# Transposing row blocks by DMA instead of on TensorE, in the prologue and in the z stage

## Chip, cores and metric
The kernel runs on one core of a Trainium2 chip. Its time is the device time of one execution in microseconds (us), lower being better. Before the change the median of three executions is 1714.83 us.

## What is computed
One transformer block on x (2048 x 512, float32): layer norm, 32-head attention (16 columns a head) with a residual, then layer norm and a gated MLP whose gate mixes over the sequence. `_A_ref` is the attention, `_B_ref` the MLP:

```python
qkv = transpose((x @ wqkv).reshape(B, S, 3, H, Dh), 2, 0, 3, 1, 4)   # x here is layernorm(x)
p = softmax(einsum("bhqd,bhkd->bhqk", q, k) * Dh ** -0.5, axis=-1)
o = einsum("bhqk,bhkd->bhqd", p, v)          # then @ wo, and h = x + ...
...
z = gelu(einsum("bsd,df->bsf", x, w_in))     # x here is layernorm(h)
z1 = z[..., :Fh]                             # Fh = 688
z2 = layernorm(z[..., Fh:], axis=-1)
g = einsum("ts,bsf->btf", w_sp, z2) + b_sp[None, :, None]
return einsum("bsf,fd->bsd", z1 * g, w_out)  # and h + ... is the result
```

## The kernel before
Products that need more precision than fp16 run as three fp16 matmuls: each operand is split in a high and a low fp16 half, and `mm3` (L106 to L109) multiplies high by high, high by low and low by high. A 128-row block of an operand therefore has to be there transposed and in two halves.

The span has four stages. The **prologue** (0 to about 165 us) loads x in 16 row blocks (`load_x`), takes statistics on DVE (`stats`), works out the scales (`scales`: one 1/sqrt chain for four blocks, ending in `nb`), normalizes on ACT (`normal`, L412), transposes on TensorE (`turn_only`, L424: four 128x128 transposes a block into PSUM) and splits (`put_x`: ACT copies the high half, L433, DVE subtracts the low half, L431). xT holds the halves. `proj_v(sb)` projects one block to v (12 matmuls of 0.216 us, 2.6 us) and `proj_qk(0, g, t)` four blocks to a q or k part; their results are taken by DVE or ACT during the next projection and stored by SyncE (v_scr, k_scr, q_scr, uv_scr). The loop over g = 0, 1, 2 treats blocks 4 to 15 in fours: it projects v of blocks 4g to 4g+3 and readies blocks 4g+4 to 4g+7. `load_q` loads the first q rows for attention (qst, six DMAs); `load_wqk` loads weights (wg).

**Attention** (about 165 to 1294 us) runs 512 units n of scores, exponentials and weighted sums; h for the first rows is made in its last units. **z** (about 1294 to 1452 us) goes over the 16 rows (blocks) in the order `h_rows`; in iteration k TensorE makes h of row k+2 (`make_h`, L747, 12 matmuls), then z of row k (`make_z`, 48 matmuls through `mm3`), with four transposes of LN(h) of row k+1 (`turn`, L1177) among them, which ACT (L98) and DVE (L104) split. `load_o` (L723, L726, L729) loads attention's output o, the softmax's 1/sums rc and the row xr of x; POOL multiplies o by rc (L731), ACT and DVE split it (`split_o`, L737, L740). h lands in xr (L751) and is stored in h_scr (L752). LN(h) is hn: applied by ACT (L1271) with scale and bias from a 1/sqrt chain (`rstd_of` with one column, L114 to L126). LN of z's second half has a chain of its own in `gate_z`, after which ACT applies it (L1214) and ACT, POOL and DVE write the sums and halves that the final stage multiplies (`parts`). The **final stage** (about 1452 to 1712 us) multiplies by w_sp and w_out.

In the prologue, attention and z, `manual_schedule` makes program order the order of each engine's queue. All DMAs that SyncE and ACT issue rotate over eight semaphores, so that a DMA waits, at its issue, for the one eight places earlier. Everything queued behind a waiting instruction on its engine waits with it.

Of the kernel before, what the change touches and what calls it, by code (L numbers as in the profile page):

```python
# [19 lines left out]
P = 128  # L20
S = 2048
# [38 lines left out]
def block_kernel(ctx: ExitStack, tc: tile.TileContext, x, wqkv, wo, w_in, w_sp4, b_sp, w_out, out):  # L60
# [208 lines left out]
    with ExitStack() as pre:  # L269
# [7 lines left out]
        xT = [pc.tile([P, DB, S], F16, name=f"xT{i}") for i in range(2)]  # L277
# [148 lines left out]
        def put_x(sb, *which):  # L426

            c = slice(sb * P, (sb + 1) * P)
            for i in which:
                if i:  # L430
                    nc.vector.tensor_sub(xT[1][:, :, c], tps[sb], xT[0][:, :, c])  # L431
                else:
                    nc.scalar.activation(xT[0][:, :, c], tps[sb], AF.Copy)  # L433

        def turn_x(*blocks):

# [175 lines left out]
        for g in range(3):  # L612
            a, b = 4 * g, 4 * g + 4
            mv = moments(4)
            if g:
                proj(proj_v, a)
                turn_x(a + 2, a + 3)
                if g == 1:
                    load_x(14)
                    load_x(15)  # L620
                stats(mv, b, b + 1)
                proj(proj_v, a + 1)
                stats(mv, b + 2, b + 3)
                proj(proj_v, a + 2)
                normal = scales(mv)
                normal(b, b + 1)
                proj(proj_v, a + 3)
            else:
                proj(proj_v, 2, on_act=True)
                stats(mv, 4, 5, 6)  # L630
                measures.pop(0)()
                stats(mv, 7)
                put_wqk(0)
                proj(proj_v, 3, on_act=True)
            if g == 1:
                load_q(0)
            proj(proj_qk, 0, g, 1)
            if not g:
                normal = scales(mv)
                normal(b, on="dve")  # L640
                normal(b + 1)
            if g == 2:
                load_wqk(1)
            proj(proj_qk, 0, g, 0, then=lambda: turn_x(b, b + 1), at=1 if g else 2)
            if not g:
                load_x(12)
                load_x(13)
            normal(b + 2, b + 3)
        weigh_wqk(1)
        proj(proj_v, 12)  # L650
        turn_x(14, 15)
        load_wqk(2)
        load_wqk(3)
        measures.pop(0)()
# [61 lines left out]
    os_, o2s, xrs, hns, hTs = {}, {}, {}, {}, {}  # L716

    def load_o(sb):

        c = slice(sb * P, (sb + 1) * P)  # L720
        o = e2.tile([P, DB, P], F32, name="o")
        for d in range(DB):
            nc.sync.dma_start(o[:, d, :], o_scr[d, :, :DH, c])  # L723
        rc = e2.tile([P, DB, P], F32, name="rc")
        for d in range(DB):
            nc.sync.dma_start(rc[:, d, :], r_scr[8 * d:8 * d + 8, c].rearrange(  # L726
                "h (o s) -> h o s", o=1).to_broadcast([8, DH, P]))
        xrs[sb] = e2.tile([P, D], F32, name="xr", bufs=3)
        nc.sync.dma_start(xrs[sb], x[c, :])  # L729
        os_[sb] = o  # L730
        return lambda: nc.gpsimd.tensor_mul(o, o, rc)  # L731

# [27 lines left out]

    def new_hn(sb):
        mv, rs = scale_h(sb)
        hns[sb] = e2.tile([P, D], F32, name="hn", bufs=3)
        nc.vector.tensor_scalar(hns[sb], xrs.pop(sb), mv[:, 0:1], rs, op0=ALU.subtract, op1=ALU.mult)

    def minus_mean(pool, mv, rs):
        nb = pool.tile([P, 1], F32, name="nb")
# [20 lines left out]
    with ExitStack() as at:  # L788
# [256 lines left out]
        for n in range(0, len(units), 2):  # L1045
# [85 lines left out]
                invert()  # L1131
            if n in (474, 484, 504, 508):
                asked.append(load_o(h_rows[{474: 0, 484: 1, 504: 2, 508: 3}[n]]))
            if n in (484, 492, 508):
                asked.pop(0)()
            if len(later) == 1 or n in (498, 510):
# [2 lines left out]
                steps_h.append(make_h(h_rows[1], later[0].tile([P, 512], F32, name="h")))  # L1139
            if n == 502:  # L1140
                new_hn(h_rows[0])
        weigh(*prev)
        take(*prev[:2], e2)
        asked.append(load_o(h_rows[4]))
# [21 lines left out]
    with ExitStack() as mid:  # L1166
        m2 = mid.enter_context(tc.tile_pool(name="mid_2", bufs=2))
        zs, zst = {}, {}
        ps = mid.enter_context(tc.tile_pool(name="mid_ps", bufs=5, space=PSUM))
        pt = mid.enter_context(tc.tile_pool(name="mid_pt", bufs=2, space=PSUM))  # L1170

        def turn(sb):

            hn = hns.pop(sb)
            tp = pt.tile([P, DB, P], F32, name="tp")
            for d in range(DB):
                nc.tensor.transpose(tp[:, d, :], hn[:, d * P:(d + 1) * P], ident)  # L1177
            hTs[sb] = [m2.tile([P, DB, P], F16, name=f"hT{i}") for i in range(2)]
            split(hTs[sb][0], hTs[sb][1], tp, "act")

        def new_z(sb):
            zs[sb] = [m2.tile([P, FH], F32, name=f"z{i}", bufs=1 + 3 * i) for i in range(2)]
# [17 lines left out]
            else:  # L1200
                sub(nc.gpsimd if el == "pool" else nc.vector)

        subs, put_off = [], []

        def gate_z(sb, meanwhile):

            z = zs.pop(sb)
            rows = slice(sb * P, (sb + 1) * P)
            nc.scalar.dma_start(z_scr[rows, :], z[0])
            mv = m2.tile([P, 2], F32, name="zmv")  # L1210
            nc.vector.bn_aggr(mv, zst.pop(sb))
            rs = rstd_of(m2, mv[:, 1:2], 1, up=Z2_UP)
            nb = minus_mean(m2, mv, rs)
            nc.scalar.activation(z[1], z[1], AF.Identity, bias=nb, scale=rs)  # L1214
            zs[sb] = z[1]
            meanwhile()
# [12 lines left out]
            t2 = m2.tile([P, FC], F32, name="t2", bufs=1)  # L1229
            e.tensor_sub(t2, b22, t1)  # L1230
            parts("t2", k, t2, eh, el)
            parts("b22", k, b22, "pool" if last else "act", "pool")
            nc.gpsimd.tensor_sub(b12, b22, b12)
            parts("t3", k, b12, "pool", "pool")
            parts("b21", k, b21, "pool" if last else "act", "pool" if last else "later")
            nc.gpsimd.tensor_sub(t2, b21, t2)
            parts("n4", k, t2, "pool", "pool")

        row = dict(enumerate(h_rows))
        with tc.manual_schedule(engines={E.PE, E.Activation, E.DVE, E.Pool, E.SP}):  # L1240
            asked.pop(0)()
            turn(row[0])
            new_hn(row[1])
            for k in range(NB):
                sb, new = row[k], row.get(k + 2)
                if new is not None:
                    for _ in make_h(new, ps.tile([P, 512], F32, name="acc")):
                        pass
                if k + 3 < NB:
                    split_o(row[k + 3])  # L1250
                new_z(sb)
                make_z(sb, 1, 0)
                if k + 1 < NB and k != NB - 2:
                    turn(row[k + 1])
                if new is not None:
                    mv, rs = scale_h(new)
                    nb = minus_mean(e2, mv, rs)
# [11 lines left out]
                if new is not None:  # L1269
                    hns[new] = e2.tile([P, D], F32, name="hn", bufs=3)  # L1270
                    nc.scalar.activation(hns[new], xrs.pop(new), AF.Identity, bias=nb, scale=rs)  # L1271
                if k == 1:
                    invert()
                if k >= NB - 8:
                    ask()

                def meanwhile(k=k):
                    if k + 4 < NB:
                        asked.pop(0)()
                    if k + 5 < NB:  # L1280
                        asked.append(load_o(row[k + 5]))

                if k == NB - 3:
                    put_off.append(lambda sb=sb, then=meanwhile: gate_z(sb, then))
                else:
                    gate_z(sb, meanwhile)
    early.close()
    late.close()

# [314 lines left out]
```

## Time and profile before

| | |
|---|---|
| median of three runs (lowest, highest) | 1714.83 us (1714.73, 1715.37) |
| span of the profiled execution | 1712.3 us |
| its own time | not listed apart from the span; the median lies 2.5 us above the span |
| granted TensorE clock, whole span | 1.000 |
| prologue / attention / z / final stage | about 165 / 1129 / 158 / 260 us |
| busy: PE, DVE, ACT, POOL | 1699.5, 1452.5, 1317.5, 813.6 us |

The profile counts an engine as busy while an instruction of it runs; matmuls overlap, so that of a run of matmuls the distance between starts is the price. A row of the waits says who waited, at which line, for whom, and for how long in total, how many times, and the longest. SPq is SyncE's queue: the time in which it issues a DMA, not the transfer.

### The profile page before, as it was taken

Reading aid. Unit: us, or ns where it says so; the run is one execution under the profiler, and the core shown is the slowest. Engines: PE = TensorE matmul, PEld = TensorE weight load, DVE = VectorE, ACT = ScalarE, POOL = GpSimd, SP = SyncE. Lnnn points to the kernel's source line nnn. Section 1 sums busy time; section 2 is a strip of 40 time slices with the busy share of each in tenths; the row PEclk is TensorE's granted clock in tenths of the full one; section 3 lists DMA queues with packets and bytes.
Section 4 is the critical chain, followed back from the end, with each engine's and each line's share of the span. In section 5 each row is a group of like instructions: output and inputs, shape, how many; then the busy total and the mean of one; then the engine's idle time right before and its main releaser. Section 6 shows DMA issues by size and latency. Waiting matters only on the chain.

```text
span 1712.3 us, 36689 instructions
## 1 busy us (share of the span) xinstructions
PE 1699.5 (99%) x13508; PEld 644.7 (38%) x13508; DVE 1452.5 (85%) x3051; ACT 1317.5 (77%) x2584; POOL 813.6 (48%) x1062
## 2 busy tenths in 40 slices
PE   9999999999999999999999999999999999999999
PEld 4533222222222222222222222222225666656665
DVE  7688999999999999999999999999936787543444
ACT  4334999999999999999999999999995545211111
POOL 1231867776673267687767776400002766300100
PEclk9999999999999999999999999999999999999999
DMA  5534332342221244344434444300114454664551
GB/s 185 167 94 144 103 89 68 101 94 82 81 68 25 56 118 117 104 144 125 130 113 124 132 140 130 80 13 19 37 39 124 140 173 140 233 234 156 198 217 44
DMA packets 189309, 196.03 MB, mean 114 GB/s; under 512 B 67496, under 2 KB 140008, under 8 KB 189128
## 3 DMA queue, kind: packets, MB, share of 16 engines
q1 hardware_dynamic: 186824, 188.04, 36.8%
q10 hardware_dynamic: 2304, 5.64, 0.8%
q8 instruction: 106, 1.74, 0.4%
q14 instruction: 75, 0.61, 0.1%
HBM read 122.10 MB, written 65.93 MB: 110 GB/s over the span
## 4 chain that ended last, share of the span: by engine, by line
PE 78%; DVE 12%; DMA 3%; POOL 2%; ACT 2%; SPq 2%; issue 1%; ACTq 0%; POOLq 0%; DVEq 0%
PE pv L830 26%; PE s L805 17%; PE m L223 9%; DVE mx L228 7%; PE acc L107 4%; PE g L108 4%; PE g L109 4%; PE g L107 4%; PE acc L109 4%; PE acc L108 4%; DMA rc<-r_scr 1%; DVE ab L237 1%; DVE og L840 1%; SPq L723 1%; DVE rs_t L124 1%
## 5 line engine op out<-in xcount | busy, mean ns | idle before, releaser
L814 ACT ACTIVATE pt<-s 128x512 f32<-128x512 f32 x1968 | 1006.2, 637 | 5.5 <-PE m L223 4.3
L228 DVE TENSOR_REDUCE mx<-m 128x1 f32<-128x512 f32 x1510 | 947.5, 682 | 11.7 <-PE m L223 2.9
L805 PE MATMUL s<-qst,kst 50*128 50x512 f16 x2048 | 604.2, 379 | 0.2
L830 PE MATMUL pv<-pt,vst 128*32 128x256 f32 (+1 forms) x6056 | 598.1, 466 | 4.1 <-DVE og L840 1.3
L223 PE MATMUL m<-kst,qst 48*128 48x512 f16 x1510 | 452.4, 381 | 0.0
L805 PEld LDWEIGHTS <-kst 50*128 50x128 f16 x2048 | 132.0, 94 | 352.1 <-issue 323.7
L830 PEld LDWEIGHTS pv<-pt,vst 128*32 128x32 f32 x6056 | 119.5, 108 | 290.7 <-issue 277.3
L223 PEld LDWEIGHTS <-qst 48*128 48x128 f16 x2048 | 159.2, 93 | 173.6 <-issue 124.2
L223 PE MATMUL m<-uvs,qst 48*128 48x512 f16 x504 | 190.5, 380 | 0.6 <-DVE mx L228 0.6
L245 POOL TENSOR_SCALAR nm<-nm 128x16 f32<-128x16 f32 x32 | 6.6, 206 | 358.8 <-DVE nm L242 358.8
L237 DVE CUSTOM_DVE_ANT_0 ab<-m,ab 128x512 f32<-128x512 f32 x252 | 170.5, 677 | 2.7 <-ACT ab L233 2.7
L233 ACT ACTIVATE ab<-m 128x512 f32<-128x512 f32 x252 | 157.3, 624 | 15.5 <-PE m L223 14.8
L1368 ACT ACTIVATE pr<-pr,up 128x304 f32<-128x304 f32 (+1 forms) x32 | 17.0, 574 | 109.2 <-DVE up L1322 109.2
L991 POOL TENSOR_TENSOR op<-raw,op 128x512 f16<-128x512 f32 x80 | 92.9, 1161 | 6.0
L914 POOL TENSOR_TENSOR raw<-raw 128x512 f32<-128x512 f32 (+1 forms) x84 | 83.3, 991 | 6.7
L919 POOL TENSOR_TENSOR acc_sp<-acc_sp,raw 128x512 f32<-128x512 f32 x63 | 80.4, 1277 | 4.5
L109 PE MATMUL acc<-wi,hT 128*128 128x344 f16 x256 | 79.1, 309 | 0.3 <-DVE hT L104 0.3
L107 PE MATMUL acc<-wi,hT 128*128 128x344 f16 x256 | 79.1, 309 | 0.0
L108 PE MATMUL acc<-wi,hT 128*128 128x344 f16 x256 | 79.1, 309 | 0.0
L1510 POOL TENSOR_TENSOR pr<-pr,z 128x344 f32<-128x344 f32 x8 | 7.3, 914 | 145.9 <-DMA whole<-squares 108.3
L911 POOL TENSOR_SCALAR raw<-raw 128x512 f32<-128x512 f32 (+1 forms) x88 | 52.3, 594 | 19.7 <-DMA raw<-in_wqkv 12.4
L1509 DVE TENSOR_TENSOR pr<-g,v 128x344 f32<-128x344 f32 x8 | 4.1, 517 | 66.6 <-PE g L109 63.5
(247 smaller groups left out, 2292.9 us busy)
## 6 DMA issues: line engine op xcount, KB each, us to landing
raw<-in_w_sp SPq DMA_DIRECT2D x128, 256.0 KB
s_scr<-op SPq DMA_DIRECT2D x64, 256.0 KB
op<-s_scr SPq DMA_DIRECT2D x32, 512.0 KB
a_scr<-op SPq DMA_DIRECT2D x48, 256.0 KB
op<-a_scr SPq DMA_DIRECT2D x24, 512.0 KB
o_scr<-og SPq DMA_DIRECT2D x64, 128.0 KB
qst<-q_scr SPq DMA_DIRECT2D x192, 32.0 KB
kst<-k_scr SPq DMA_DIRECT2D x48, 128.0 KB
```

Source lines behind the costliest of these rows:

```text
L107: nc.tensor.matmul(ps, lh, rh, start=first, stop=False, **kw)
L108: nc.tensor.matmul(ps, lh, rl, start=False, stop=False, **kw)
L109: nc.tensor.matmul(ps, ll, rh, start=False, stop=last, **kw)
L223: nc.tensor.matmul(acc, q[r, p, c], keys[r, p], start=True, stop=True)
L228: nc.vector.reduce_max(at(t, e if t else e - 1), acc, axis=AX.X)
L233: nc.scalar.activation(ab[0], acc, AF.Abs)
L237: nc.vector.tensor_tensor_reduce(ab[0], acc, ab[0], 0.5, LOW, ALU.add, ALU.max, at(0, 0))
L805: nc.tensor.matmul(s, kst[hg % 2][r, p, kb * P:(kb + 1) * P], qst[hg * NQ + qb][r, p, :], start=True, stop=True)
L814: nc.scalar.activation(pts[p, kb][:, t, :], s, AF.Exp, scale=scales_[hg // 2])
L830: nc.tensor.matmul(pv[0][32 * j:32 * j + 32, a:b], vst[hg % 2][:, c:c + 32], pts[j % 2, kb][:, j // 2, a:b], start=kb == 0, stop=kb == NB - 1,
L914: pool.tensor_mul(got[0] if n else acc, got[0], got[0])
L991: chores.append((lambda: pool.tensor_sub(t[0][:, 1], of(), t[0][:, 0]), TT))
```

## The change
In the prologue blocks 8 to 15 are no longer transposed on TensorE. ACT copies the normalized block into the first half of an fp16 tile xp, POOL subtracts for the second half, and one transposing DMA, issued by SyncE, writes all eight 128x128 pieces into xT (`split_x`). The statistics come as three blocks and one, and the scales ahead of proj_v(a + 2); `load_wqk(1)` moves to the start of g = 2.

In z the same is done to LN(h): `halve_h` copies (ACT; DVE for the first row), `turn_h` subtracts on DVE and issues the transposing DMA into hT. Row 0's is done at unit n = 504 of attention, row 1's ahead of the loop, row k+1's at the start of iteration k. One chain, `scale_both`, serves z of row k and h of row k+2. The gate of row k−1 comes in iteration k, z's first half is stored right after it is made, xr is loaded by itself, and the z matmuls have seven PSUM buffers instead of five.

```diff
+        def split_x(*blocks):
+            for sb in blocks:
+                xn = xns.pop(sb)
+                xp = p2.tile([P, 2, D], F16, name="xp", bufs=4)
+                nc.scalar.activation(xp[:, 0], xn, AF.Copy)
+                nc.gpsimd.tensor_sub(xp[:, 1], xn, xp[:, 0])
+                nc.sync.dma_start_transpose(
+                    xTs[:, :, :, sb * P:(sb + 1) * P].rearrange("p i d s -> p (i d) s"),
+                    xp.rearrange("p i c -> p (i c)"))
...
             if g:
+                if g == 2:
+                    load_wqk(1)
                 proj(proj_v, a)
-                turn_x(a + 2, a + 3)
                 if g == 1:
+                    turn_x(a + 2, a + 3)
                     load_x(14)
                     load_x(15)
-                stats(mv, b, b + 1)
+                stats(mv, b, b + 1, b + 2)
                 proj(proj_v, a + 1)
-                stats(mv, b + 2, b + 3)
+                stats(mv, b + 3)
+                normal = scales(mv)
+                for sb in (b, b + 1):
+                    normal(sb)
+                    split_x(sb)
                 proj(proj_v, a + 2)
-                normal = scales(mv)
-                normal(b, b + 1)
+                for sb in (b + 2, b + 3):
+                    normal(sb)
+                    split_x(sb)
                 proj(proj_v, a + 3)
...
+    def turn_h(sb):
+        hp = hps.pop(sb)
+        nc.vector.tensor_sub(hp[:, 1], hns.pop(sb), hp[:, 0])
+        t = e2.tile([P, 2 * DB, P], F16, name="hT")
+        nc.sync.dma_start_transpose(t, hp.rearrange("p i c -> p (i c)"))
+        hTs[sb] = [t[:, :DB], t[:, DB:]]
...
             for k in range(NB):
                 sb, new = row[k], row.get(k + 2)
+                if k and k + 1 < NB:
+                    nb, rs = scaled.pop(row[k + 1])
+                    hns[row[k + 1]] = e2.tile([P, D], F32, name="hn")
+                    nc.scalar.activation(hns[row[k + 1]], xrs.pop(row[k + 1]), AF.Identity, bias=nb, scale=rs)
+                    halve_h(row[k + 1])
+                    turn_h(row[k + 1])
...
+                if k:
+                    gate_z(row[k - 1])
                 new_z(sb)
                 make_z(sb, 1, 0)
-                if k + 1 < NB and k != NB - 2:
-                    turn(row[k + 1])
...
                 make_z(sb, 1, 1)
-                if k == NB - 2:
-                    turn(row[k + 1])
-                    put_off.pop()()
                 for c in range(2):
                     nc.vector.bn_stats(zst[sb][:, c, :], zs[sb][1][:, c * FC:(c + 1) * FC])
+                scale_both(new, sb)
                 make_z(sb, 0, 0)
                 make_z(sb, 0, 1)
+                nc.scalar.dma_start(z_scr[sb * P:(sb + 1) * P, :], zs[sb][0])
```

The order on SyncE's queue in the prologue, from the last load of x on; names are destination and source (v_scr, k_scr, q_scr and uv_scr are stores of projections, qst attention's first rows of q, wg weights). Before:

```order
L286 DMA xg<-in_x 128x512 x2
L493 DMA v_scr<-v 128x512 x3
L194 DMA qst<-q_scr 16x2x512 x6
L493 DMA v_scr<-v 128x512
L464 DMA k_scr<-part 128x2x512
L481 DMA uv_scr<-part 64x2x512 x2
L464 DMA q_scr<-part 128x2x512
L493 DMA v_scr<-v 128x512 x4
L345 DMA wg<-in_wqkv 128x4x128 x2
```
The same queue after, from the same place on:

```order
L505 DMA v_scr<-v 128x512
L443 DMA_TRANSPOSE xT<-xp 128x8x128 x2
L505 DMA v_scr<-v 128x512
L443 DMA_TRANSPOSE xT<-xp 128x8x128 x2
L505 DMA v_scr<-v 128x512
L194 DMA qst<-q_scr 16x2x512 x6
L505 DMA v_scr<-v 128x512
L476 DMA k_scr<-part 128x2x512
L346 DMA wg<-in_wqkv 128x4x128 x2
L493 DMA uv_scr<-part 64x2x512 x2
L476 DMA q_scr<-part 128x2x512
L505 DMA v_scr<-v 128x512
```
Four transposing DMAs (blocks 8 to 11) now stand ahead of qst, and those of blocks 12 to 15 follow the last row shown, in two pairs with a v_scr between.

SyncE's queue in one iteration of z, before:

```order
L752 DMA h_scr<-xr 128x512
L723 DMA o<-o_scr 128x1x128 x4
L726 DMA rc<-r_scr 128x1x128 x4
L729 DMA xr<-in_x 128x512
L752 DMA h_scr<-xr 128x512
```
and after:

```order
L799 DMA_TRANSPOSE hT<-hp 128x8x128
L772 DMA h_scr<-xr 128x512
L738 DMA xr<-in_x 128x512
L745 DMA o<-o_scr 128x1x128 x4
L748 DMA rc<-r_scr 128x1x128 x4
L799 DMA_TRANSPOSE hT<-hp 128x8x128
```
The transposing DMA stands first in the iteration, and xr has moved ahead of o and rc.

ACT's queue in one iteration of z (tp is the transposes' PSUM, acc the z matmuls', fig a scale), before:

```order
L737 ACTIVATE o_20883<-o,fig_1844 128x512
L1192 ACTIVATE z_20888<-acc,fig_1841 128x344
L98 ACTIVATE hT_20909<-tp 128x512
L1192 ACTIVATE z_20888<-acc,fig_1841 128x344
L1192 ACTIVATE z_20887<-acc,fig_1841 128x344 x2
L1271 ACTIVATE hn<-xr,nb,rs_u 128x512
L1214 ACTIVATE z_20888<-z_20888,nb,rs_u 128x688
```
and after:

```order
L1296 ACTIVATE hn<-xr,nb_21163,r_21161 128x512
L790 ACTIVATE hp<-hn 128x512
L757 ACTIVATE o_21229<-o,fig_1819 128x512
L1261 ACTIVATE z_21122<-z_21122,nb_21163,r_21161 128x688
L1226 CAST b_0_20646<-z_21122 128x344
L1226 CAST b_0_20644<-z_21122 128x344
L1222 ACTIVATE z_21260<-acc,fig_1816 128x344 x2
L1222 ACTIVATE z_21259<-acc,fig_1816 128x344 x2
L1324 DMA z_scr<-z_21259 128x688
```
hn and its copy now open the iteration, the gate of the row before follows, and the store of z's first half, issued by ACT, closes it.

More of the change, by code (lines that the diff above doesn't have):

```diff
@@ L275, in block_kernel @@
         more[3] = more[4] = lambda: pt.tile([P, 512], F32, name="tp")
-        xT = [pc.tile([P, DB, S], F16, name=f"xT{i}") for i in range(2)]
+        xTs = pc.tile([P, 2, DB, S], F16, name="xT")
+        xT = [xTs[:, i] for i in range(2)]
         wv = [pc.tile([P, DB, D], F16, name=f"wv{i}") for i in range(2)]
@@ L637, in block_kernel @@
             proj(proj_qk, 0, g, 1)
-            if not g:
+            if g:
+                proj(proj_qk, 0, g, 0)
+            else:
                 normal = scales(mv)
@@ L641, in block_kernel @@
                 normal(b + 1)
[L642 to L645, printed above, removed]
+                proj(proj_qk, 0, g, 0, then=lambda: turn_x(b, b + 1), at=2)
                 load_x(12)
                 load_x(13)
-            normal(b + 2, b + 3)
+                normal(b + 2, b + 3)
         weigh_wqk(1)
         proj(proj_v, 12)
-        turn_x(14, 15)
         load_wqk(2)
@@ L715, in block_kernel, with load_row @@
     h_rows = [0, 1, HB, HB + 1] + [sb + HB * i for sb in range(2, HB) for i in range(2)]
-    os_, o2s, xrs, hns, hTs = {}, {}, {}, {}, {}
+    os_, o2s, xrs, hns, hps, hTs = {}, {}, {}, {}, {}, {}
+    def load_row(sb):
+        xrs[sb] = e2.tile([P, D], F32, name="xr", bufs=3)
+        nc.sync.dma_start(xrs[sb], x[sb * P:(sb + 1) * P, :])
     def load_o(sb):
@@ L762, in new_hn, with halve_h @@
         mv, rs = scale_h(sb)
-        hns[sb] = e2.tile([P, D], F32, name="hn", bufs=3)
+        hns[sb] = e2.tile([P, D], F32, name="hn")
         nc.vector.tensor_scalar(hns[sb], xrs.pop(sb), mv[:, 0:1], rs, op0=ALU.subtract, op1=ALU.mult)
+    def halve_h(sb, on_act=True):
+        hps[sb] = e2.tile([P, 2, D], F16, name="hp")
+        if on_act:
+            nc.scalar.activation(hps[sb][:, 0], hns[sb], AF.Copy)
+        else:
+            nc.vector.tensor_copy(hps[sb][:, 0], hns[sb])
+    def turn_h(sb):
[4 more added lines that the diff above has]
+        hTs[sb] = [t[:, :DB], t[:, DB:]]
     def minus_mean(pool, mv, rs):
@@ L1168, in block_kernel @@
         zs, zst = {}, {}
[L1169 to L1179, printed above, removed]
+        ps = mid.enter_context(tc.tile_pool(name="mid_ps", bufs=7, space=PSUM))
         def new_z(sb):
@@ L1201, in parts, with scale_both, gate_z @@
                 sub(nc.gpsimd if el == "pool" else nc.vector)
[L1203 to L1213, printed above, removed]
+        subs = []
+        def scale_both(new, sb):
+            n = 1 if new is None else 2
+            mv = m2.tile([P, 2, 2], F32, name="mv2")
+            hv = m2.tile([P, 2], F32, name="hv2")
+            for i, (row, stats, up) in enumerate(((sb, zst, Z2_UP), (new, hst, HN_UP))[:n]):
+                nc.vector.bn_aggr(mv[:, i, :], stats.pop(row))
+                nc.vector.tensor_scalar(hv[:, i:i + 1], mv[:, i, 1:2], EPS, 0.5 / up ** 2,
+                                        op0=ALU.add, op1=ALU.mult)
+            r, t, nb = [m2.tile([P, 2], F32, name=f"{i}_2")[:, :n] for i in ("r", "t", "nb")]
+            hv = hv[:, :n]
+            nc.vector.tensor_scalar(r.bitcast(I32), hv.bitcast(I32), -0.5, GUESS,
+                                    op0=ALU.mult, op1=ALU.add)
+            for _ in range(3):
+                nc.vector.tensor_mul(t, r, r)
+                nc.vector.tensor_mul(t, t, hv)
+                nc.vector.scalar_tensor_tensor(r, t, 1.5, r, op0=ALU.subtract, op1=ALU.mult)
+            nc.vector.scalar_tensor_tensor(nb, mv[:, :n, 0], -1.0, r, op0=ALU.mult, op1=ALU.mult)
+            for i, row in enumerate((sb, new)[:n]):
+                scaled[row] = nb[:, i:i + 1], r[:, i:i + 1]
+        scaled = {}
+        def gate_z(sb):
+            z, (nb, rs) = zs.pop(sb), scaled.pop(sb)
             nc.scalar.activation(z[1], z[1], AF.Identity, bias=nb, scale=rs)
             zs[sb] = z[1]
-            meanwhile()
             if sb < HB:
@@ L1250, in block_kernel @@
                     split_o(row[k + 3])
+                if k + 4 < NB:
+                    load_row(row[k + 4])
+                if k + 5 < NB:
+                    asked.append(load_o(row[k + 5]))
+                if k >= NB - 8:
+                    ask()
+                if k:
+                    gate_z(row[k - 1])
                 new_z(sb)
                 make_z(sb, 1, 0)
-                if k + 1 < NB and k != NB - 2:
-                    turn(row[k + 1])
-                if new is not None:
-                    mv, rs = scale_h(new)
-                    nb = minus_mean(e2, mv, rs)
                 if subs:
@@ L1260, in block_kernel @@
                 make_z(sb, 1, 1)
-                if k == NB - 2:
-                    turn(row[k + 1])
-                    put_off.pop()()
                 for c in range(2):
                     nc.vector.bn_stats(zst[sb][:, c, :], zs[sb][1][:, c * FC:(c + 1) * FC])
+                scale_both(new, sb)
                 make_z(sb, 0, 0)
                 make_z(sb, 0, 1)
+                nc.scalar.dma_start(z_scr[sb * P:(sb + 1) * P, :], zs[sb][0])
                 hTs.pop(sb)
-                if new is not None:
-                    hns[new] = e2.tile([P, D], F32, name="hn", bufs=3)
-                    nc.scalar.activation(hns[new], xrs.pop(new), AF.Identity, bias=nb, scale=rs)
                 if k == 1:
                     invert()
[L1274 to L1286, printed above, removed]
+            gate_z(row[NB - 1])
     early.close()
```

11 lines of the change are left out of this document (8 added, 3 removed).

## The prediction
> **What bounds the kernel now.** I read the page's first part first, then the busy time by stretches of the span, then the waits of TensorE and SyncE, then the order in time at the places that the change touches.
>
> ```profile
> PE 1699.5 (99%) x13508; PEld 644.7 (38%) x13508; DVE 1452.5 (85%) x3051; ACT 1317.5 (77%) x2584; POOL 813.6 (48%) x1062
> ```
> The share of 99% says that TensorE hardly stands still; the stretches say which engines stand beside it (columns: stretch, PE, PEld, DVE, ACT, POOL busy, granted clock, DMA share, GB/s).
>
> ```profile
> 40.00:60.00 20.00, 20.00 (x102) 10.14 (x101) 13.87 (x43) 7.35 (x12) 3.04 (x3) 1.00 0.35 116
> 60.00:80.00 20.00, 20.00 (x103) 10.32 (x101) 11.44 (x22) 7.36 (x12) 6.35 (x10) 1.00 0.60 188
> 600.00:1250.00 650.00, 647.00 (x5850) 183.63 (x5851) 644.31 (x1245) 648.53 (x1319) 365.43 (x473) 1.00 0.35 101
> 1294.00:1460.00 166.00, 165.24 (x1056) 103.17 (x1054) 128.79 (x411) 84.47 (x149) 100.64 (x118) 1.00 0.49 150
> ```
> Attention (third row) has PE, DVE and ACT all full, and the change leaves it alone. In the prologue (first two rows) and in z (last row) TensorE alone is full at a granted clock of 1.00: there, work taken off TensorE shortens the span as long as nothing makes it wait. Between 1286 and 1460 it waits twice in all:
>
> ```profile
> PE acc L109 <- DVE hT L104: 0.3, 1, 0.3
> PE acc L747 <- DVE og L840: 0.2, 1, 0.2
> ```
>
> **TensorE's transposes: the gain.** In z, one row block's transposes stand between two z matmuls:
>
> ```profile
> 1314.50 2.75 PE L747 MATMUL acc<-wo,o 128*128 128x512 f16 x12
> ...
> 1318.69 0.31 PE L109 MATMUL acc<-wi,hT 128*128 128x344 f16 x1
> 1318.84 0.60 PE L1177 MATMUL tp<-ident,hn 128*128 128x128 f32 x4
> 1319.27 0.31 PE L107 MATMUL acc<-wi,hT 128*128 128x344 f16 x1
> ...
> 1324.52 1.67 PE L747 MATMUL acc<-wo,o 128*128 128x512 f16 x7
> ```
> Starts, not durations, give the price, since matmuls overlap: 1319.27 − 1318.84 = 0.43 us for four. An iteration lasts 1324.52 − 1314.50 = 10.02 us and becomes 9.59. There are 16 such groups; the first lies ahead of the only wait for og, which ends where it ended, so 15 x 0.43 = 6.5 us come off.
>
> In the prologue a pair of x's row blocks costs:
>
> ```profile
> 46.05 1.04 PE L424 MATMUL tp<-ident,xg 128*128 128x128 f32 x8
> 46.92 0.38 PE L107 MATMUL acc<-xT,wqk 128*128 128x512 f16 x1
> ...
> 48.22 0.38 PE L107 MATMUL acc<-wv,xT 128*128 128x512 f16 x1
> ...
> 65.50 0.38 PE L107 MATMUL acc<-wv,xT 128*128 128x512 f16 x1
> ```
> 46.92 − 46.05 = 0.87 us; four pairs, 3.5 us. At the end of z TensorE waits once for a low half from POOL, put off behind another row's gate:
>
> ```profile
> 1454.63 0.31 PE L107 MATMUL g<-b,op 128*128 128x344 f16 x1
> 1455.04 0.31 PE L108 MATMUL g<-b,op 128*128 128x344 f16 x1
> ```
> The step is 0.41 us where a matmul takes 0.15; the new order gates the row before at the start of the next iteration, so I take off 0.3. Sum if all else is hidden: 6.5 + 3.5 + 0.3 = 10.3 us.
>
> **What a transposing DMA costs.** Each moves 128x1024 fp16, 256 KB, and none is in this trace. Two quantities matter: x, the time it holds SyncE's queue, and L, from then until it has landed. Nearest rows of SyncE, from the order in time in z and from the final stage's source line:
>
> ```profile
> 1333.96 2.48 SPq L723 DMA_DIRECT2D o<-o_scr  x4
> 1336.50 2.44 SPq L726 DMA_DIRECT2D rc<-r_scr  x4
> 1339.35 0.33 SPq L729 DMA_DIRECT2D xr<-in_x  x1
> 1342.20 0.33 SPq L752 DMA_DIRECT2D h_scr<-xr  x1
> L1397 SPq DMA_DIRECT2D whole<-squares x112: 507/589/1131, 1481.7 to 1682.3; - x112
> ```
> h_scr is a plain store of the same 256 KB: 0.33 us, the low end. The high end is the kernel's other transpose by DMA: 16 issues of 48 KB for a pair of blocks (112 in seven pairs), 16 x 0.589 = 9.4 us for 768 KB, so 3.1 us for 256 KB. One instruction should cost less than the five issues which that stands for, yet its pattern is much finer than a plain store's; I take the middle, x = 1.7 us (an estimate). For L, two rows of the chain of waits:
>
> ```profile
> 866.40 2.46 DMA s_scr<-op
> 1409.90 5.17 DMA rc<-r_scr
> ```
> A 256 KB store lands 2.46 us after it was issued, about 2.1 beyond its issue; a load among many took 5.17. I take L = 2.5 and keep 2.1 to 4.8.
>
> The Trainium skill, "VectorE: DVE Perf Modes", section "The three transpose paths", speaks against this change: it lists 1309 ns for a 128x128 bf16 block by DMA against 390 ns on TensorE, and a row block here is eight such blocks. By it the sum would be 8 x 1.309 = 10.5 us for one transposing DMA, an estimate from that page, and the last rival would come true. This trace has TensorE's side alone, 0.43 us for four fp32 blocks.
>
> **z: is it hidden?** An iteration has 2.48 + 2.44 + 0.33 + 0.33 = 5.6 us of issues. SyncE's own waits there:
>
> ```profile
> SPq L752 <- DVE xr L751: 36.9, 10, 10.0
> ```
> They are waits for work, not for room: 9.59 − 5.6 leaves 4.0 us per iteration, so x = 1.7 fits. In the queue each transposing DMA stands ahead of h_scr, xr, o and rc; behind it o and rc come 1.7 us later, but they are used two iterations on. Where it waits for its source, that row's chain matters: hn, its copy on ACT, the subtraction on DVE.
>
> ```profile
> L1271 ACT ACTIVATE hn<-xr,nb,rs_u 128x512 f32<-128x512 f32 x14 | 11.4, 811 | 19.5 <-DVE nb L768 19.5
> L98 ACT ACTIVATE hT<-tp 128x512 f16<-128x512 f32 x16 | 9.4, 585 | 1.8 <-PE tp L1177 1.8
> L104 DVE TENSOR_TENSOR hT<-tp,hT 128x512 f16<-128x512 f32 x16 | 11.1, 692 | 4.7 <-ACT hT L98 4.0
> L124 DVE TENSOR_SCALAR rs_t<-rs_u,rs_v 128x1 f32<-128x1 f32 x62 | 16.9, 273 | 2.2
> ```
> From an iteration's start that is 0.81 + 0.59 + 0.69, with hops and a DVE in use some 2.9 us; the first matmul that reads it is due 9.59 + 2.6 = 12.2 us after that start. So x + L may reach 9.3 and is 4.2: hidden by 5 us. The copies and subtractions replace L98 and L104 one for one. Two 1/sqrt chains of some 2.2 us (the 0.27 of L124 is the longest of ten steps) become one of two columns; DVE is busy 128.8 of 166 us and holds nobody up, so I count nothing for it, as for the seven PSUM buffers, xr's own issue and z_scr's earlier store (this on ACT's queue can wait for the DMA eight places earlier, an o; its lateness comes out of the same 5 us). Row 0's copy, subtraction and DMA go into attention's last units, where DVE has room:
>
> ```profile
> 1250.00:1294.00 44.00, 43.96 (x307) 9.00 (x306) 11.28 (x25) 41.66 (x49) 4.46 (x6) 1.00 0.20 55
> ```
>
> **The prologue: here the cover is thin.** Taking out transposes also makes TensorE arrive earlier. proj_v(8) began at 48.22 and, one pair less, is due at 47.35; proj_v(12) at 65.50 − 3 x 0.87 = 62.9; the last projections that read blocks 14 and 15 began at 71.99, due at 68.5.
>
> ```profile
> 71.99 0.38 PE L107 MATMUL acc<-xT,wqk 128*128 128x512 f16 x1
> 42.68 0.16 DVE L401 SCALAR_TENSOR_TENSOR nb<-mv,rs_r 128x4 f32<-128x4 f32 x1
> 42.92 1.52 ACT L412 ACTIVATE xg<-xg,nb,rs_r 128x512 f32<-128x512 f32 x2 [7.68 <-issue]
> L433 ACT ACTIVATE xT<-tp 128x512 f16<-128x512 f32 x16 | 8.8, 594 | 7.7 <-PE tp L424 7.6
> 25.84 1.16 POOL L319 TENSOR_TENSOR wqk<-wg,wqk 128x512 f16<-128x512 f32 x1
> 43.95 4.30 SPq L194 DMA_DIRECT2D qst<-q_scr x6
> 39.86 0.73 DVE L492 TENSOR_SCALAR v<-acc,v 128x512 f32<-128x512 f32 x1
> ```
> Block 8: nb ends at 42.84; with the statistics' new order it stands ahead of one v copy (0.73), so 42.1. Then 0.76 normalizing, 0.6 copying (ACT), 1.16 subtracting (POOL, 3.0 of 20 us busy): 44.6. Landed at 44.6 + x + L = 48.8 against 47.35: **TensorE waits 1.5 us**. Blocks 9 to 11 follow at x each, while TensorE takes 2.6 per proj_v: no more waits. Call block n's transposing DMA Tn. For T12 to T15 SyncE first issues v_scr(6), the six qst (4.30), two v_scr, k_scr, two wg, two uv and q_scr (some 4 together): with T8 to T11 from 44.6 on it is free for T12 at 53.3 + 4x = 60.1 or when the source is there, 59.7. T15 lands at 55.6 − 2 + 8x + L = 69.7 against 68.5 plus the 1.5 already waited: hidden. In general the wait is the larger of x + L − 2.75 and 8x + L − 14.9. The POOL subtractions, 8 x 1.16, have room; ACT's copies stand ahead of the take of a k block by 2.6 us, whose PSUM bank is wanted at about 50: at most 0.3 more, inside L's bounds. The two wg loads that move ahead of T12 are two issues, in the 4 above.
>
> At x = 0.33, L = 2.1 the prologue waits 0; at x = 1.7, L = 4.8, 3.8; at x = 3.1, L = 2.5, 12.4.
>
> **Sum.** −10.3 + 1.5 = −8.8 us. The sum is against the profiled execution, of which the trace gives the span, 1712.3 us; the median of the three runs, 1714.83, lies 2.5 above and contains what stands around the span, which I take as unchanged: 1706.0.
>
> **Rivals.**
> - All hidden: x under about 0.6, or sources ready sooner. Only the 10.3 show: 1704.5. For it: the 0.33 of a plain 256 KB store.
> - It doesn't pay: at x between 2.4 and 3.3 the prologue's wait, 8x + L − 14.9, eats the gain: at 3.1 it is 12.4, so +2.1, 1716.9; at 2.9, +0.5, 1715.3. TensorE's time then falls in z by 6.5 and stands as idle time ahead of blocks 11, 12 and 15. For it: the whole<-squares row.
> - Slower: SyncE's queue becomes the bound. From x = 3.3 on the prologue's wait exceeds the gain by over 3.4, and from 4.0 on z runs at the queue's pace too, 5.6 + x. At x = 5: the prologue waits 27.6, 14 iterations of 10.6 instead of 10.02 add 8 in place of saving 6.5, less 3.5 + 0.3: some +32, 1747. Against it: no issue in the trace takes over 1.2 us (1131 ns is the largest of 112).
>
> The skill's section above belongs to this last one: its eight blocks would put x + L, in the queue or in flight, far over both bounds.
>
> **How the numbers follow.** The likeliest case, x from 0.6 to 2.3, has 0.42; all hidden 0.25; eaten up 0.15; slower 0.18. A measurement of this kernel tells about 0.2% (3.4 us) from no change, so faster 0.67, same 0.15, slower 0.18. The range goes from 1703.5 (all hidden and a little ACT or DVE relief) to 1717.0, the end at x = 3.1; the likeliest case's own range is 1704.5 to 1711.
>
> **What would show it.** z's iterations start every 9.6 us and no PE row L1177 is left; SyncE's row of a transposing DMA gives x; the waits of PE in the prologue name that DMA for proj_v(8), and little or nothing for 12 to 15. I am wrong if x is far from 1.7, if z's period stays near 10, naming a wait for the transposed h, or if attention or the final stage changes length, which nothing here predicts.

## The result, and the profile after

The changed kernel takes 1725.57 us (median; 1725.45 to 1726.57) against 1714.83 for the kernel before in the same comparison: ratio 1.0064, 95% interval 1.0053 to 1.0075. It is 10.7 us slower, where 8.8 us faster was forecast. The span of the profiled execution is 1723.7 us, 11.4 more than before. First the page's first part and the stretches, columns as before.

```profile
PE 1695.4 (98%) x13412; PEld 634.6 (37%) x13412; DVE 1452.3 (84%) x2980; ACT 1321.1 (77%) x2583; POOL 819.6 (48%) x1070
```

```profile
40.00:60.00 20.00, 19.29 (x89) 8.53 (x88) 12.37 (x40) 9.56 (x15) 8.02 (x8) 1.00 0.56 140
60.00:80.00 20.00, 18.13 (x85) 8.42 (x83) 8.25 (x16) 5.80 (x10) 10.66 (x14) 1.00 1.07 273
1294.00:1460.00 166.00, 153.17 (x926) 90.89 (x921) 127.06 (x329) 81.29 (x141) 93.58 (x112) 0.97 0.63 164
```

TensorE has 96 matmuls fewer in the records, as meant, and yet it stood idle for 12.8 us of the z stretch, where before it stood 0.8; the granted clock there is 0.97 on average instead of 1.00. Its waits from the end of attention on:

```profile
PE acc L767 <- DVE o L760: 6.1, 4, 2.5
PE acc L107 <- DMA hT<-hp: 5.0, 4, 3.1
PE acc L767 <- DVE rs_v L114: 1.8, 1, 1.8
PE g L107 <- POOL t L1227: 0.7, 1, 0.7
```

L767 is the h product, which waits for the split of o; L107 on hT is z, which waits for the transposing DMA. By places: attention starts 0.35 us sooner (161.90 before, 161.55 now); from there to z's first h product it takes 2.3 us more (1132.55, 1134.87); z takes 9.0 more (1294.45 to 1451.57 before, 157.1; 1296.42 to 1462.51 now, 166.1); and at its end a step of 1.00 us from one matmul to the next (1462.20 to 1463.20, with the wait of 0.7 in it) stands where one of 0.41 stood. The final stage is as long as it was. Since the forecast for z was 150.6 us (157.1 − 6.5), z lost 15.5 us against the forecast.

The three waits of over 2 us cost twice. Behind each of them the granted clock is one half for 3.4 us (the seventh number after the stretch):

```profile
1348.70:1352.10 3.40, 3.40 (x10) 1.18 (x8) 3.23 (x9) 0.00 (x0) 3.26 (x5) 0.50 0.42 136
1382.83:1386.24 3.41, 3.41 (x11) 1.48 (x10) 2.97 (x14) 0.00 (x0) 1.86 (x3) 0.50 0.55 190
1447.69:1451.09 3.40, 3.40 (x14) 1.82 (x12) 1.30 (x5) 2.59 (x4) 0.24 (x1) 0.50 0.45 178
```

Half of 3 x 3.4 is 5.1 us; 6.1 + 5.0 + 5.1 = 16.2, near the 15.5. What made o's split and hT late is in DVE's order in time, here with POOL's instructions among them (start, duration, engine and line; one iteration of z):

```profile
1325.90 1.27 POOL L751 TENSOR_TENSOR o<-o,rc 128x512 f32<-128x512 f32 x1 [4.42 <-DVE mv L1241]
1326.03 1.16 DVE L1246 TENSOR_SCALAR r<-hv 128x2 int32<-128x2 int32 x1
1327.13 0.84 POOL L1227 TENSOR_TENSOR b<-z,b 128x344 f16<-128x344 f32 x1
1327.23 0.75 DVE L1249 TENSOR_TENSOR t<-r 128x2 f32<-128x2 f32 x1
1328.02 0.16 DVE L1250 TENSOR_TENSOR t<-t,hv 128x2 f32<-128x2 f32 x1
1328.05 0.91 POOL L1266 TENSOR_TENSOR z<-z 128x344 f32<-128x344 f32 x1
1328.21 0.76 DVE L1251 SCALAR_TENSOR_TENSOR r<-t,r 128x2 f32<-128x2 f32 x1
...
1330.87 0.16 DVE L1252 SCALAR_TENSOR_TENSOR nb<-mv,r 128x2 f32<-128x2 f32 x1
1331.07 0.82 ACT L1296 ACTIVATE hn<-xr,nb,r 128x512 f32<-128x512 f32 x1 [4.96 <-DVE nb L1252]
```

These are two columns of 128 numbers. Where POOL is between two instructions, a step takes 0.16 us (L1250 at 1328.02). Where POOL is inside one, the step ends with it: 1326.03 + 1.16 = 1327.19 against 1325.90 + 1.27 = 1327.17; 1327.23 + 0.75 = 1327.98 against 1327.13 + 0.84 = 1327.97; 1328.21 + 0.76 = 1328.97 against 1328.05 + 0.91 = 1328.96. The chain, from L1246 to L1252, takes 5.0 us here instead of 2.2, and behind it hn waits, and behind hn on ACT's queue its copy, o's split, the gate and z's results:

```profile
ACT hn L1296 <- DVE nb L1252: 56.2, 11, 7.5
```

The longest wait for hT is of this kind too: its hn began only at 1440.43, SyncE issued the DMA at 1442.70, and z went on at 1446.66.

In the prologue the transposing DMA was priced about right, and yet its gain went. First the view of its source line (minimum, median, maximum in ns), then TensorE's order in time, then SyncE's:

```profile
L443 SPq DMA_TRANSPOSE xT<-xp x8: 1239/1304/1865, 45.2 to 67.1; - x8
```

```profile
43.07 0.38 PE L107 MATMUL acc<-xT,wqk 128*128 128x512 f16 x1 [0.71 <-DVE v L504]
...
65.99 0.39 PE L107 MATMUL acc<-wv,xT 128*128 128x512 f16 x1 [1.87 <-DMA xT<-xp]
```

```profile
61.37 3.52 SPq L443 DMA_TRANSPOSE xT<-xp  x2
```

It holds SyncE 1.30 us (the median; in z 1.28). TensorE waits 0.7 us at 43.07 for a PSUM bank (the memory that takes a matmul's result), whose v copy stands behind the 1/sqrt chain on DVE, and 1.9 us at 65.99 for block 12, whose DMA was issued at 61.37 and landed some 4.5 us later.

### The profile page after: what moved, and what is told of

Read it like the earlier page. It is cut to its first block, busy times and chain, and to the rows that moved or that the text cites. A ratio compares the mean times of both kernels' runs of the same rounds, so it can differ in the third digit from the quotient of the medians.

```text
span 1723.7 us, 36473 instructions
## 1 busy us (share of the span) xinstructions
PE 1695.4 (98%) x13412; PEld 634.6 (37%) x13412; DVE 1452.3 (84%) x2980; ACT 1321.1 (77%) x2583; POOL 819.6 (48%) x1070
## 4 chain that ended last, share of the span: by engine, by line
PE 72%; DVE 14%; POOL 4%; DMA 3%; issue 2%; ACT 2%; SPq 2%; POOLq 0%; ACTq 0%
PE pv L866 24%; PE s L841 17%; PE m L223 9%; DVE mx L228 7%; PE g L107 4%; PE g L108 4%; PE g L109 4%; PE acc L107 3%; PE acc L109 3%; PE acc L108 3%; DVE ab L237 1%; DVE og L876 1%; DMA rc<-r_scr 1%; SPq L745 1%; DMA raw<-in_w_sp 1%
## 5 line engine op out<-in xcount | busy, mean ns | idle before, releaser
L233 ACT ACTIVATE ab<-m 128x512 f32<-128x512 f32 x252 | 158.7, 630 | 15.5 <-PE m L223 14.8
L107 PE MATMUL acc<-wi,hT 128*128 128x344 f16 x256 | 80.4, 314 | 5.0 <-DMA hT<-hp 5.0
L751 POOL TENSOR_TENSOR o<-o,rc 128x512 f32<-128x512 f32 x16 | 20.3, 1270 | 109.6 <-DMA rc<-r_scr 55.5
```

The source lines that it names most:

```text
L107: nc.tensor.matmul(ps, lh, rh, start=first, stop=False, **kw)
L233: nc.scalar.activation(ab[0], acc, AF.Abs)
```

## The experiments

Theory A: the joint chain makes z late, since its instructions stretch beside POOL and stand between z's statistics and the next hn. Theory B: the transposing DMAs make it late by themselves. Times below are against the kernel before on the same chip, whose median was 1713.06 to 1713.47 us there.

**Two one-operand chains, h's early.**

```diff
                 if k + 3 < NB:
                     split_o(row[k + 3])
...
+                if new is not None:
+                    scale_new(new)                # rstd_of, one column, behind h's statistics
...
-                scale_both(new, sb)
+                scale_z(sb)                       # rstd_of, one column, behind z's statistics
```

> The changed kernel with its one two-column 1/sqrt chain in z taken apart again: h's one-column chain right behind h's statistics, z's behind z's statistics, with the one-operand instructions of the kernel before; the transposing DMAs, the order and the prologue stay. Theory A (the joint chain stands between z's statistics and the next hn, and its two-input instructions last 0.6 us instead of 0.16 beside POOL, so that hn, the split of o and the transposing DMA come late): TensorE's waits for the split of o (6.1 us) and for hT (5.0) and the three stretches at half clock (1.7 each) go, z lasts 150 to 153 us instead of 166, and the time is 1709 to 1713. Theory B (the transposing DMAs themselves hold up z: their transfers crowd the loads of o and rc and land late): the waits stay, 1720 to 1727.

Measured: 1712.26 us, ratio 0.9993 (0.9983 to 1.0003): the loss is gone. No wait for the split of o is left; z takes 158.5 us, where 150 to 153 were expected. Two waits for hT of 1.3 us and more remain, all in its last third; TensorE's waits, and the stretch at half clock behind the longest:

```profile
PE acc L107 <- DMA hT<-hp: 7.0, 3, 5.2
```

```profile
1418.03:1424.85 6.82, 5.01 (x18) 2.72 (x19) 4.20 (x12) 4.80 (x9) 3.40 (x5) 0.50 0.84 273
```

That speaks for A in most of it, but this run changed the chain's place and the kind of its instructions at once; the next runs tell these apart, and the rest called for another theory (the load, below).

**The same places, two-input instructions.** `tensor_mul(t, r, r)`, `tensor_mul(t, t, hv)` and `scalar_tensor_tensor` on one column in place of `tensor_scalar` with column scalars.

> As the run with two chains, h's early, but both chains written with the two-input instructions of the joint chain, on one column each. It tells the place of h's chain from the kind of its instructions. Theory A1 (the kind decides: each chain lasts 2.2 us alone and 4 to 5 beside POOL, and DVE, now with two of them, is late again): 1718 to 1730. Theory A2 (the place decides: once hn doesn't wait for z's statistics, DVE's longer chains are hidden): 1709 to 1714. Theory B: 1720 to 1727 as well, so this run tells A1 from A2 only if the run with two one-operand chains is fast.

Measured: 1735.1 us, ratio 1.0129 (1.0112 to 1.0146), z 177.2 us, TensorE waiting 13.0 us for the split of o and 7.8 for hT. That is above even the 1730 of the range for A1. The place did not save it: of the same two chains in the same places, the one-operand kind is 22.8 us faster.

**One part alone.** The kernel before with only the prologue's edits, and with only z's.

> The kernel before with the prologue's part of the change alone. From the changed kernel's trace: attention's first weighted sum 0.2 to 0.6 us sooner than before, so the time 1714 to 1715, no change that can be told. If attention's slower pace in the changed kernel's profile (1.35 us over 1091 us, evenly) comes from the prologue's new tiles and where they lie, it shows here too: 1715 to 1716.5. If the waits of 0.7 and 2.0 us in the prologue were chance, 1711 to 1712.

> The kernel before with z's part of the change alone (row 0 in attention's last units included). If z alone makes the loss: 1723 to 1727, z 166 us with the same waits for the split of o and for hT. If the prologue's transposing DMAs or attention's pace carry part of it, less: 1718 to 1722.

Measured: prologue alone 1712.65, ratio 0.9999 (0.9989 to 1.0008); z alone 1723.64, ratio 1.0062 (1.0045 to 1.0079), z 166.5 us. The whole loss is z's, and the prologue's part is worth nothing measurable. Attention, unchanged in all, took between 1131.9 us (z alone) and 1134.1 (prologue alone) from its first weighted sum to z's first h product, so the changed kernel's 1134.87 there is mostly the spread of profiles; only the last wait ahead of z (on DVE, 1.8 us here and 0.8 with z alone, where 0.2 stood) is the change's. The start of attention spreads as well: it came at 161.06 with the prologue alone and, with an unchanged prologue, at 162.38 with z alone, against 161.90 before, so the 0.35 us above can't be told from nothing.

**The joint chain in its place, one-operand instructions.**

```diff
...
-                nc.vector.tensor_mul(t, r, r)
-                nc.vector.tensor_mul(t, t, hv)
-                nc.vector.scalar_tensor_tensor(r, t, 1.5, r, op0=ALU.subtract, op1=ALU.mult)
+                for i in cols:
+                    nc.vector.tensor_scalar(t[:, i], r[:, i], r[:, i], hv[:, i], op0=ALU.mult, op1=ALU.mult)
+                for i in cols:
+                    nc.vector.tensor_scalar(u[:, i], t[:, i], 1.5, r[:, i], op0=ALU.subtract, op1=ALU.mult)
+                r, u = u, r
...
```

> The changed kernel with its joint chain left in its place, but each step written as two one-column, one-operand instructions (0.27 and 0.21 us each) in place of one two-column, two-input instruction (0.16, or 0.6 beside POOL). The chain then lasts some 4.5 us whatever POOL does, where in the changed kernel it lasted 4 to 5.5. If what counts is how long hn waits behind z's statistics (length and place): 1718 to 1726, little or nothing gained. If the stretched instructions alone did the harm (kind): 1708 to 1714.

Measured: 1713.26, ratio 1.0000 (0.9990 to 1.0009). So the kind of instruction alone takes back the 10.7 us, and the rest of z's change (the seven PSUM buffers, xr's own issue, z_scr's earlier store), which is still in this run, didn't make the loss. The expectation that the length would stay was wrong: two columns' steps, one behind the other, overlap, and a pair takes 0.45 and 0.33 us:

```profile
1345.27 0.46 DVE L1251 TENSOR_SCALAR t<-r,hv 128x1 f32<-128x1 f32 x2
1345.64 0.33 DVE L1253 TENSOR_SCALAR u<-t,r 128x1 f32<-128x1 f32 x2
1346.25 0.33 DVE L1253 TENSOR_SCALAR r<-t,u 128x1 f32<-128x1 f32 x2
```

The chain lasts 2.5 us beside POOL, and DVE is busy 112.6 us in the z stretch instead of 127.1. Kind and length can't be told apart here: the kind sets the length.

**POOL nearly idle.**

```diff
-            (nc.gpsimd.tensor_copy if eh == "pool" else nc.scalar.copy)(T[name][0][:, k, :], src)
+            nc.scalar.copy(T[name][0][:, k, :], src)
+            if el == "pool":
+                nc.vector.tensor_copy(T[name][1][:, k, :], src)
+                return
...
-                nc.gpsimd.tensor_sub(b1, b2, b1)
+                nc.gpsimd.tensor_sub(b1[:, :FEW], b2[:, :FEW], b1[:, :FEW])     # FEW = 8
```

> The changed kernel, joint two-input chain and all, with POOL kept nearly idle in z: it leaves out the gate's subtractions on POOL (full halves become copies, made by ACT and DVE; differences are taken over 8 of 344 columns), so the output isn't the reference's, and TensorE, the DMAs and the order stay. POOL keeps the product of o by 1/sums. DVE gets copies in exchange. If POOL beside them is what stretches the chain's instructions: they last 0.16 us but for those beside the product of o, the chain 2.2 to 3.2 us, the waits for the split of o and most of those for hT go, and the time is 1709 to 1716 where the changed kernel needs some 1724. If the two-column, two-input instructions are slow in themselves: 1720 or more and the same 0.6 us.

Measured: 1730.88, ratio 1.0102 (1.0085 to 1.0118). The instructions do what the expectation says; rows of groups by form in z (two of a chain's three repeated steps), the changed kernel's first, then this kernel's, then ACT's waits in this kernel:

```profile
L1249 DVE TENSOR_TENSOR t<-r 128x2 f32<-128x2 f32 x42 | 16.2, 385 | 1.5
L1251 DVE SCALAR_TENSOR_TENSOR r<-t,r 128x2 f32<-128x2 f32 x42 | 14.5, 345 | 1.5
```

```profile
L1252 DVE TENSOR_TENSOR t<-r 128x2 f32<-128x2 f32 x42 | 6.8, 161 | 1.4
...
L1254 DVE SCALAR_TENSOR_TENSOR r<-t,r 128x2 f32<-128x2 f32 x42 | 6.8, 161 | 1.5
```

```profile
ACT t L1226 <- POOL z L1269: 20.2, 8, 7.3
ACT t L1226 <- DVE t L1279: 12.0, 7, 2.7
```

The 42 of each take 161 ns on average: POOL was the cause of the stretch. The time missed: it lies in the other theory's range, which these rows rule out. The copies moved to ACT and DVE made ACT's queue wait 32 us for POOL and DVE, ahead of z's results, so this run says nothing on what the chain is worth.

**The big load moved behind the transposing DMA.** On top of the two early chains:

```diff
                     turn_h(row[k + 1])
+                if k >= NB - 8:
+                    ask()                         # 512 KB for the final stage
...
-                if k >= NB - 8:
-                    ask()
```

> The run with two one-operand chains, h's early, and one move more: the 512 KB load for the final stage (op, one per iteration in the last eight) is issued right behind the transposing DMA instead of 2 to 4 us ahead of the next one. In the profile of the run without the move, TensorE waited three times for hT in these iterations, 7.0 us in all, one DMA taking 9.3 us from its issue to its landing, and one stretch of 6.8 us at half clock cost 3.4 more. Theory C (the transposing DMA is overtaken by nothing and stands behind a big load in the DMA engines): the waits for hT go, z lasts 150 to 152 us and the time is 4 to 9 us below the kernel before. Rival (the transposing DMA is slow in itself when o, rc and z_scr are in flight): the waits stay, within 2 us of the kernel before.

Measured: 1706.88, ratio 0.9963 (0.9950 to 0.9977), 6.5 us faster than before. z takes 150.8 us, the forecast's 150.6, and of the waits for hT this is left:

```profile
PE acc L107 <- DMA hT<-hp: 1.3, 2, 0.7
```

**Each transposing DMA of z twice.**

> As the run with the op load behind the transposing DMA, but each of z's 16 transposing DMAs is issued a second time, into a tile that nobody reads. It prices the transposing DMA itself: SyncE's queue then has 5.6 + 2 x 1.3 = 8.2 us of issues in an iteration of 9.6. If the transposing DMA is cheap beside z's work, within 3 us of the run without the second one. If the DMA engines are near their limit in z (the theory that its transfers crowd out o, rc and z_scr): 8 us slower or more, with waits for hT and for the split of o.

Measured: 1723.96, ratio 1.0065 (1.0050 to 1.0080): 17 us more than without the second, z 15.4 us longer.

```profile
PE acc L107 <- DMA hT<-hp: 9.6, 7, 1.9
PE acc L767 <- DVE o L760: 5.1, 7, 1.0
```

One per iteration is hidden, a second is not: B is right in so far as there is no room for more of them. The second took SyncE 1.82 us in the median, so an iteration's issues come to 5.6 + 1.28 + 1.82 = 8.7 us of 9.6: the queue alone doesn't set the pace, but it is near its end. Which of the queue, the engines that move the data and the landing behind other transfers gives out first stays open.

**The prologue mended.** v of block 5 taken by ACT, statistics and scales of blocks 12 to 15 one loop sooner, the qst loads behind the last transposing DMA:

```diff
-                proj(proj_v, a + 1)
+                    proj(proj_v, a + 1, on_act=True)
...
             if g == 1:
+                mv = moments(4)
+                stats(mv, 12, 13, 14, 15)
+                proj(proj_qk, 0, g, 0)
+                normal = scales(mv)
+            elif g:
                 load_q(0)
```

> The kernel before with the prologue's part of the change, mended in three places: v of block 5 is taken by ACT, so that its PSUM bank doesn't wait for DVE's 1/sqrt chain (0.7 us); the statistics and scales of blocks 12 to 15 come one loop sooner; the six qst loads go behind the last transposing DMA (with these two, block 12 should land before 60 us instead of at 65.9, where TensorE waited 1.9). If these are the prologue's only waits: attention starts 2.5 to 3.2 us sooner than in the kernel before and the time is 2 to 3 us below it. If the earlier statistics make DVE late for the takes of q and k: within 1 us of it.

Measured: 1710.86, ratio 0.9985 (0.9976 to 0.9994). Attention starts at 159.60 instead of 161.90; of the prologue's waits on the change one is left, 1.0 us for block 8.

**Both mended parts, and the same with the joint one-operand chain.**

> Both mended parts together: z with two one-operand chains and the op load behind the transposing DMA (alone 6.5 us below the kernel before, with the unmended prologue), and the mended prologue (alone 2.5 us below, where the unmended one was at 0.4 below). If the two are independent: 6.5 + 2.1 = 8.6, with 1.5 either way, so 7 to 10 us below the kernel before. If attention or the z stage absorbs an earlier start: 6 to 7.

> As the run before it, but with the joint chain in the changed kernel's place, its steps as pairs of one-column, one-operand instructions (in the run that changed this alone a chain lasted 2.5 to 2.7 us, and DVE was busy 112.6 us in z in place of 130.8). If hn's wait for z's statistics costs nothing at that length: within 2 us of the two-chain version, 6 to 10 us below the kernel before. If h's early chain matters: 2 to 5 us slower than it, with waits for hT.

Measured: 1706.22, ratio 0.9957 (0.9944 to 0.9971), the fastest of all, 7.3 us below the kernel before; with the joint chain 1708.42, ratio 0.9968 (0.9956 to 0.9980), and 3.8 us of waits for hT against 1.4. The two versions' intervals overlap, so whether h's early chain matters isn't shown; the interval of the run with z's part alone mended (0.9950 to 0.9977) overlaps with the first as well. Of the sum of the parts (8.6) 1.3 is missing; that lies within the spread of attention in the profiles and wasn't followed further.

## Why the prediction was wrong

**The step that failed** is "Two 1/sqrt chains ... become one of two columns; DVE is busy 128.8 of 166 us and holds nobody up, so I count nothing for it ..." Two things were wrong in it. The joint chain is not the price of one chain: the one-column steps of before (L124, L126) read one tensor and take their scalars by column, and all 96 of L124 lasted 272 to 275 ns beside the same POOL; the joint one's read two, and they stretch to 0.6 us and more beside POOL, which was busy 100.6 of 166 us in the very row quoted. And DVE's share of busy time was taken for its slack, although the new order puts hn, the head of ACT's queue, behind that chain's end. The Trainium skill, "SBUF — State Buffer", section "Who interferes with whom", says that a VectorE instruction with two SBUF inputs contends with a GpSimd instruction that reads SBUF, and one with a single input doesn't, outside the two-port modes. The trace agrees for the two-input steps and for L124; the prediction should have weighed it. The one-input L1246 stretched as well, to 1.16 us on two columns, while the same step on one column took 153 to 155 ns each of 30 times in the run with two-input chains; whether it ran in a two-port mode no run here shows.

**z's cover, "hidden by 5 us".** x + L was about right (4.2 assumed; some 4.5 for block 12, about 3.2 for block 8), but the start of it was not. The prediction let hn begin with the iteration. Here is an iteration's first matmul and its hn:

```profile
1334.78 2.92 PE L767 MATMUL acc<-wo,o 128*128 128x512 f16 x12
...
1342.86 0.81 ACT L1296 ACTIVATE hn<-xr,nb,r 128x512 f32<-128x512 f32 x1 [6.18 <-DVE nb L1252]
```

That is 8.1 us late, more than the cover. Even in the run with the load moved hn came mostly 3.6 to 5.7 us after its iteration's start (1364.70 after 1361.12, 1405.20 after 1399.48), so that little of the 5 us is left; z has the forecast's length there because the 512 KB load stands behind the DMA. That load was missed: in the run with two early chains it was issued at 1406.95, and a transposing DMA issued behind it at 1410.30 let z start only at 1419.84. These 9.5 us are more than the 1.7 + 4.8 that the prediction kept as the most for x + L.

**The price x.** 1.7 us estimated, 1.28 to 1.30 measured; the queue was not the bound in the changed kernel (5.6 + 1.28 = 6.9 of 9.59 us). That the kernel came out slower, as one rival said, is not that rival's doing: the slowdown came by DVE and POOL. The estimate of eight times the 1309 ns that the Trainium skill lists for one block ("VectorE: DVE Perf Modes", "The three transpose paths") does not hold here: one DMA of eight blocks held SyncE for 1.3 us and landed in about 3.2 us (block 8) to some 4.5 (block 12).

**The prologue.** The wait for block 8 was forecast as 1.5 us and measured as less than 0.2, since TensorE had already lost 0.7 to a v copy behind the chain on DVE; "it stands ahead of one v copy" was seen as a gain of 0.73 for nb, and not as a PSUM bank given back late. Block 12 was forecast as hidden and cost 1.9: SyncE was free for it at 61.37, not 60.1, and it took 4.5 us instead of 4.2. Together 0.35 us of gain where 2.0 was forecast.

**What held:** 0.43 us for a group of four transposes (z's iterations without a wait start 9.59 us apart). The 0.87 for eight fits the mended prologue: attention starts 2.3 us sooner and 1.0 us of waiting is left, together 3.3 of 3.5. The 10.3 − 1.5 was a fair price for the idea, but not for this kernel: the mended version, with moves that the forecast didn't have, reaches 7.3.

**The end of z:** the step of 0.41 went, but one of 1.00 came for it at z's last matmul, with a wait of 0.7 that stands in every version with z's new order (0.6 in that with every DMA twice), so that −0.3 was +0.6.

## What to carry to other kernels

Before you merge small DVE steps into wider ones, look at how many tensors each reads and what POOL does beside it: a step of 0.16 us can last until POOL's instruction ends. An engine that is 78% busy has no slack to give where another's queue has been put behind its last step: follow the new order's loop once around, with the durations under contention. A DMA that is on a deadline goes ahead of the big load, not behind it; and a wait of TensorE of some 2 us or more may cost 1.7 more in clock, though not each of them did here.

## What the hardware showed

- A two-input DVE instruction on 128 x 2 numbers, and even a one-input one on two int32 columns (L1246), lasted up to 0.84 and 1.16 us, to the end of the POOL instruction that was running; one-column, one-input steps stayed at 0.14 to 0.28 us.
- The granted clock fell to 0.50 for 3.4 us behind single waits of 2.1, 2.5 and 3.1 us, and not behind those of up to 1.9 us in the run with every DMA twice; in the run of z alone, with waits of 2.25, 2.22 and 2.90, it fell behind the second only, and with POOL nearly idle it fell behind one of 1.55 and not behind one of 2.62. These runs give no threshold.
- A transposing DMA of 256 KB holds SyncE 1.3 us in the median (2.4 at most in the changed kernel), but its landing went from 3.2 to over 9 us with a 512 KB load ahead; one more per iteration of 9.6 us cost z 15.4 us.
